# A fused attention and mixture-of-experts kernel: where the small experts' first-layer sums are kept, and which engine clears the result columns

## The chip, the cores and the metric

One core of one Trainium2 chip runs the whole program. The metric is the device time of one execution in microseconds (us). The five engines are named as the profile names them: PE (TensorE; PEld is its weight load), DVE (VectorE), ACT (ScalarE), POOL (GpSimd) and SP, whose queue starts most DMAs. SBUF is the working memory, PSUM the memory that matmuls write, in banks of 512 fp32 columns.

## What is computed

Attention with RMS-normed queries and keys (4 batches, 12 heads, 448 positions, head size 64) gives 1792 tokens of 768 values. Each token goes to one of 8 experts, and a dense layer with a softmax-weighted linear unit and a layer norm follows. Cut to what matters here:

```
x = attention(q, k, v, g_q, g_k)                  # 1792 x 768
expert_idx = argmax(x @ w_gate, axis=1)
for e in range(8):
    mask = expert_idx == e
    h = np.maximum(x[mask] @ w1[e], 0.0)          # 768 -> 1024
    out[mask] = gate_w[mask, None] * (h @ w2[e])  # 1024 -> 768
h = out @ w_in                                    # 768 -> 1024
ln = layer_norm(h * softmax(h)) * g_ln
result = ln @ w_out
```

## The kernel before

The program has three stages. Attention and routing come first; their instructions are placed by a planner (class `Work`). Then come the experts, in an order written out by hand (the loop `for r in range(E_)` in `body`), and last a head that takes 14 blocks of 128 tokens. The change lies in the experts and in the seam ahead of them.

**The experts.** The experts are taken in order of their number of tokens, with fixed capacities `CAP = (192, 280, 280, 280, 256, 208, 208, 192)`. Experts 0, 5, 6 and 7 of this order have fewer than 256 columns and are the small ones; experts 1 to 4 are the large ones. Every fp32 operand is split into a high part and a remainder, and a product is made of three partial products. For a large expert the three are added in the same PSUM columns. For a small one `products` runs the high and the remainder columns side by side in one matmul, so that a sum lies in two halves of a bank, `ps[:, :n]` and `ps[:, n:2n]`, which must be added.

**One step.** An expert has 8 steps `fc`, each with one first-layer sum `h` (`layer1`, 12 matmuls for a small expert) and, one step behind, its second-layer part `y` (`layer2`, 12 matmuls into six banks). PE's order is h_0, h_1, y_0, h_2, y_1 and so on, with y_7 right behind y_6. For each small sum (lines 1194 to 1203):

- ACT copies the first half to an SBUF tile `ht` (L1196);
- DVE adds the second half from PSUM to it, into `ht` (L1197, "the add");
- `between()` puts a conversion of the next weights on ACT (`w_high`, L1109);
- ACT writes `hh`, the rectified high part, from `ht` (L1202, "the relu");
- DVE writes `hl`, the rectified remainder, from `ht` and `hh` (L1203, "the subtraction"). The second-layer matmuls read both.

For a large expert the relu and the subtraction read the bank itself.

**What shares the engines.** The remainder `wl` of each weight block (L1114) is made by DVE or, for the second-layer weights of small experts, by POOL. DVE also rebuilds fp32 numbers from int64 pairs for the head's weights (L1526, L1529, L1532), and POOL makes the remainder of the first of these (L1545). `xprep` transposes one sixth of the next expert's tokens (PE L1165), from step 2 to 7 of every expert but the last.

**Banks.** The sums and the transposes take turns in two banks of the pool `ps_h` (tag `h`). In an expert with transposes, from step 2 on, every sum therefore lies in the same bank as the sum before it. In expert 7, which has none, the sums alternate.

**The result columns.** `yT` holds the experts' results by column. Expert 0 writes its first 192 columns; the other 1704 columns of each of six rows are set to zero by POOL in steps 0 to 5 of expert 1 (L1618), since later experts write at places held in registers.

**The seam.** Between attention and expert 0, POOL starts the gather of expert 0's tokens by two indirect DMAs (`ex.gather`, L1129), PE transposes them as they land (`transpose_all`, L1175), ACT takes the high part (L1183) and DVE the remainder (L1184).

Of the kernel before, what the change touches and what calls it, by code (L numbers as in the profile page):

```python
# [12 lines left out]
ALU = mybir.AluOpType  # L13
# [13 lines left out]
def f32(ap):  # L27
    return ap.bitcast(F32)
# [618 lines left out]
CAP = (192, 280, 280, 280, 256, 208, 208, 192)  # L647
# [439 lines left out]
class Experts:  # L1087
# [98 lines left out]
    def layer1(self, w, x, n, nm, fc=0, between=None):  # L1186
        nc = self.nc
        ps = self.h_bank(f"h{nm}")
        for k in range(6):
            c = slice(k * 128, (k + 1) * 128)  # L1190
            self.products(ps, [a[:, c] for a in w], [a[:, k] for a in x], n, k == 0, k == 5)
        x = self.wk.tile([128, 2 * self.cols], F32R, tag="hh", name=f"hh{nm}", bufs=2)
        hh, hl = self.parts_tiles(x, n)
        if n < 256:
            t = self.ht[fc % 2]
            nc.scalar.copy(t, ps[:, :n])  # L1196
            nc.vector.tensor_tensor(t, ps[:, n : 2 * n], t, op=ALU.add)  # L1197
        else:
            t = ps[:, :n]
        if between and n < 256:  # L1200
            between()
        nc.scalar.activation(hh, t, AF.Relu)  # L1202
        nc.vector.scalar_tensor_tensor(hl, t, 0.0, f32(hh), op0=ALU.max, op1=ALU.subtract)  # L1203
        if between and n >= 256:
            between()
        return x, hh, hl
# [166 lines left out]
def body(tc, kq, v, g_qk, w_gate, wmoe, w_in, w_out, g_ln, out):  # L1373
    nc = tc.nc
    ctx = ExitStack()
    with ctx, tc.manual_schedule():
# [29 lines left out]
        def reg(ap, eng, hi):  # L1406
            return eng.value_load(ap, min_val=0, max_val=hi)
# [15 lines left out]
        def w_high():  # L1423
            if len(wd) < len(use):
                r, fc, half = key = use[len(wd)]
                nm = f"{r}_{fc}_{half}"
                raw = raws[key]["r"] if key in raws else ex.load(w_reg(r), fc, half, nm)
                wd[key] = raw, ex.high(raw, nm), nm

        def w_low():  # L1430
            key = use[len(wd) - 1]
            if len(wd[key]) == 3:
                raw, wh, nm = wd[key]

                e = nc.gpsimd if CAP[key[0]] < 256 and (key[2] or key[1] == 0) else nc.vector
                wd[key] = wh, ex.low(raw, wh, nm, e)
# [75 lines left out]
        yT = yp.tile([128, 6, max(min(NT, sum(CAP[:r])) + CAP[r] for r in range(E_))], F32, name="yT")  # L1512
# [24 lines left out]
        def m2_in(i):  # L1537
            f = slice(i * HC, (i + 1) * HC)
            w, fs = from_f64(w_in[:, f], f"i{i}")
            hh = wih.rearrange("p k f -> p (k f)")[:, f]  # L1540
            ll = wil.rearrange("p k f -> p (k f)")[:, f]

            def parts():
                nc.scalar.copy(hh, w)
                nc.gpsimd.tensor_tensor(ll, w, f32(hh), op=ALU.subtract)  # L1545

            return fs + [parts]

        def m2_out(i):
            kk, j = divmod(i, 2)  # L1550
            f = slice(j * HC, (j + 1) * HC)
            w, fs = from_f64(w_out[128 * kk : 128 * kk + 128, f], f"o{i}")
            return fs + [
                lambda: nc.scalar.activation(wo[:, kk, f], w, AF.Copy, scale=gl[:, kk : kk + 1])
            ]
# [2 lines left out]
        gx = {0: ex.gather(gi(0), CAP[0], "0")}  # L1558
        small = [plan.lists(cnt), plan.tail_lists()]

        def run_small(m=1):
            for _ in range(m):
                while small and next(small[0], small) is small:
                    small.pop(0)
# [3 lines left out]
        def fetch(dst, src, at, t):  # L1568
            nc.gpsimd.indirect_dma_start(
                out=dst[:, t : t + 1], out_offset=None, in_=src[:, :],  # L1570
                in_offset=bass.IndirectOffsetOnAxis(ap=at[:, t : t + 1], axis=0),
            )
# [3 lines left out]
        def xprep(r, k):  # L1576
            if k == 0:
                xs[r] = ex.xT_tiles(r, CAP[r])
            ex.transpose(gx[r], xs[r], k, CAP[r], r)
# [4 lines left out]
        for r in range(E_):  # L1584
            n = CAP[r]
            if n < 256:
                t = wk.tile([128, DM], F32, tag="gx", name=f"ht{r}", bufs=4)
                ex.ht = t[:, :n], t[:, DM // 2 : DM // 2 + n]
            if r + 1 < E_:
                gx[r + 1] = ex.gather(gi(r + 1), CAP[r + 1], r + 1)  # L1590
            if r == 2:

                idx += [lambda t=t: fetch(tok, tab, plan.slot, t) for t in range(14)]
                idx += [lambda t=t: fetch(gate, gd, tok, t) for t in range(14)]
            ys = ex.y_banks(r)

            def y_out():
                for kk in range(6):
                    o, p = yT[:, kk, bass.ds(o_v, n)], ys[kk]
                    if n < 256:  # L1600
                        nc.scalar.copy(yT[:, kk, bass.ds(o_a, n)], p[:, :n])
                        nc.vector.tensor_tensor(o, p[:, n : 2 * n], o, op=ALU.add)
                    elif kk % 2:
                        nc.scalar.copy(yT[:, kk, bass.ds(o_a, n)], p[:, :n])
                    else:
                        nc.vector.tensor_copy(o, p[:, :n])

            h_prev = None
            m2 = []
            for fc in range(9):  # L1610
                if fc < 8:
                    h = ex.layer1(wd[r, fc, 0], xs[r], n, f"{r}_{fc}", fc, w_high)
                    w_low()
                    if r:
                        run_small(8)
                    if r == 1 and fc < 6:

                        nc.gpsimd.memset(yT[:, fc, CAP[0] :], 0.0)  # L1618
                    if m2:
                        m2.pop(0)()  # L1620
                if fc > 0:
                    ex.layer2(wd[r, fc - 1, 1], h_prev, ys, n, fc - 1)
                    if fc == 8 and n < 256:
                        y_out()
                    w_high()
                    w_low()
                h_prev = h
                if r + 1 < E_ and 2 <= fc < 8:
                    xprep(r + 1, fc - 2)
                if fc in (0, 2, 4, 6):  # L1630
                    u = fc // 2
                    m2 = m2_in(4 * r + u) if r < 4 else m2_out(4 * (r - 4) + u)
                    m2.pop(0)()
                else:
                    m2.pop(0)()
                for _ in range(2):
                    if idx:
                        idx.pop(0)()
                if r == E_ - 1 and fc == 5:
                    hd = Head(nc, None, None, None, ident, (wih, wil), None, out)  # L1640

                    free = lambda nm: wk.tile([128, DM], F32, tag="gx", name=nm, bufs=4)
                    cut = lambda a: a.bitcast(F32R).rearrange("p (k n) -> p k n", k=6)
                    ysp = hd.split(yT[:, :, 0:128], 0, (cut(free("yh0")), cut(free("yl0"))))
                if fc == 4:
                    o_a, o_v = (
                        reg(plan.off_i[0:1, r : r + 1], e, min(NT, sum(CAP[:r]))) if r else 0 for e in (nc.scalar, nc.vector)
                    )
            if n >= 256:
                y_out()  # L1650
# [203 lines left out]
```

## Time and profile before

| | us |
|---|---|
| median of 3 runs | 899.03 |
| lowest and highest | 896.51, 904.44 |
| the profiled execution | 896.94 |
| its span in the profile | 895.2 |
| PE busy in it | 811.1 (91%) |
| DVE, ACT, POOL busy | 641.4, 497.8, 395.1 |

The profile is one execution. Its span is the time from the first to the last instruction; 1.7 us lie around it. The seam ends at about 336 us, expert 0 runs to 371, experts 1 to 4 to 535, experts 5 to 7 to 635, and the head to the end. In the timeline a row gives its start, its duration, engine, line, operation and operands, and in brackets how long the engine sat idle before it and what ended that.

### The profile page before, as it was taken

Reading aid. Unit: us, or ns where it says so; the run is one execution under the profiler, and the core shown is the slowest. Engines: PE = TensorE matmul, PEld = TensorE weight load, DVE = VectorE, ACT = ScalarE, POOL = GpSimd, SP = SyncE. Lnnn points to the kernel's source line nnn. Section 1 sums busy time; section 2 is a strip of 40 time slices with the busy share of each in tenths; the row PEclk is TensorE's granted clock in tenths of the full one; section 3 lists DMA queues with packets and bytes.
Section 4 is the critical chain, followed back from the end, with each engine's and each line's share of the span. In section 5 each row is a group of like instructions: output and inputs, shape, how many; then the busy total and the mean of one; then the engine's idle time right before and its main releaser. Section 6 shows DMA issues by size and latency. Waiting matters only on the chain.

```text
span 895.2 us, 18893 instructions
## 1 busy us (share of the span) xinstructions
PE 811.1 (91%) x6811; PEld 740.8 (83%) x6811; DVE 641.4 (72%) x1484; ACT 497.8 (56%) x958; POOL 395.1 (44%) x420
## 2 busy tenths in 40 slices
PE   2788998987898959989999999899899999999994
PEld 2577887776787849979999999789779989998994
DVE  7988998897898937998667778788575434444541
ACT  7787988886885805644455556667532323332221
POOL 4777898787784624543674125545110000000000
PEclk9999999999997979999999999999999999999998
DMA  7476575574743355757666777767000000000001
GB/s 207 125 200 171 134 197 145 146 197 83 198 111 83 117 118 164 222 187 244 209 220 202 260 229 250 243 211 245 2 1 36 19 36 19 18 18 36 19 18 38
DMA packets 63871, 120.29 MB, mean 134 GB/s; under 512 B 12159, under 2 KB 35290, under 8 KB 63774
## 3 DMA queue, kind: packets, MB, share of 16 engines
q1 hardware_dynamic: 60478, 107.69, 40.8%
q0 software_dynamic: 3296, 11.35, 4.0%
q8 instruction: 56, 0.92, 0.4%
q14 instruction: 41, 0.34, 0.1%
HBM read 86.08 MB, written 11.03 MB: 108 GB/s over the span
## 4 chain that ended last, share of the span: by engine, by line
PE 36%; issue 26%; DVE 17%; DMA 13%; ACT 4%; POOL 2%; SPq 1%; POOLq 0%; ACTq 0%; DVEq 0%
DMA out_dram<-ot,tok 5%; PE st L497 4%; DMA QQ<-QQ 3%; PE h L1157 3%; DVE mx L508 2%; PE h L1158 2%; PE y L1157 2%; PE h L1159 2%; PE y L1158 2%; PE y L1159 2%; PE r L497 2%; PE h L1154 2%; DMA gx<-xd,gx 2%; PE y L1154 2%; DMA rkq<-in_kq_dram 2%
## 5 line engine op out<-in xcount | busy, mean ns | idle before, releaser
L558 POOL TENSOR_TENSOR pl<-pf,ph 128x448 f16<-128x448 f32 x153 | 166.1, 1105 | 47.7 <-ACT ph L555 16.8
L1359 POOL DMA_INDIRECT out_dram<-ot,tok x14 | 13.8, 987 | 214.3 <-ACT ot L1358 208.8
L508 DVE TENSOR_REDUCE mx<-r 128x1 f32<-128x448 f32 x168 | 99.4, 611 | 12.3 <-PE r L497 11.9
L1114 POOL TENSOR_TENSOR wl<-wr,wh 128x768 fp32r<-128x768 f32 x34 | 64.5, 1899 | 93.6 <-ACT wh L1109 93.1
L1109 ACT CAST wh<-wr 128x768 fp32r<-128x768 f32 x128 | 104.7, 831 | 1.6 <-DMA wr<-in_wmoe_dram 1.6
L1114 DVE TENSOR_TENSOR wl<-wr,wh 128x768 fp32r<-128x768 f32 x94 | 97.5, 1037 | 10.5 <-ACT wh L1109 9.0
L551 ACT ACTIVATE pf<-st 128x448 f32<-128x448 f32 x168 | 86.7, 544 | 22.0 <-PE st L497 19.5
L497 PE MATMUL r<-KS,QQ 128*128 128x448 f32 x192 | 69.0, 428 | 21.0 <-DMA QQ<-QQ 12.1
L555 ACT CAST ph<-pf 128x448 f16<-128x448 f32 x153 | 82.5, 569 | 0.3
L587 PEld LDWEIGHTS <-ph 128*128 128x128 f16 x768 | 71.0, 97 | 12.0 <-issue 10.9
L587 PE MATMUL av<-va,ph 128*128 128x65 f16 x768 | 80.1, 194 | 0.0
L588 PE MATMUL av<-va,ph 128*128 128x64 f16 x768 | 79.7, 195 | 0.0
L589 PE MATMUL av<-va,pl 128*128 128x65 f16 x768 | 79.3, 193 | 0.0
L497 PE MATMUL st<-QQ,KS 128*128 128x448 f32 x192 | 74.4, 408 | 2.7 <-ACT pf L551 2.6
L1320 DVE TENSOR_TENSOR cl<-ct,ch 128x512 fp32r<-128x512 f32 x28 | 18.1, 686 | 80.3 <-ACT ch L1319 80.2
L589 PEld LDWEIGHTS <-pl 128*128 128x128 f16 x768 | 71.6, 99 | 0.0
L588 PEld LDWEIGHTS <-ph 128*128 128x128 f16 x768 | 71.4, 97 | 0.1
L497 PE MATMUL st<-Q,K 128*128 128x448 f32 x192 | 68.7, 378 | 0.5 <-DMA K<-KS 0.5
L1154 PE MATMUL y<-hh,wh 128*128 128x384 f32 (+1 forms) x192 | 61.0, 354 | 7.7 <-DVE hh L1203 7.4
L1154 PE MATMUL h<-xx,wh 128*128 128x384 f32 (+1 forms) x192 | 63.0, 364 | 0.4 <-DVE xx L1184 0.4
L497 PEld LDWEIGHTS r<-KS,QQ 128*128 128x128 f32 x192 | 35.5, 199 | 31.1 <-DVE mx L508 5.9
L1157 PE MATMUL h<-xx,wh 128*128 128x280 f32 (+1 forms) x192 | 57.4, 299 | 0.7 <-DVE hh L1203 0.7
(282 smaller groups left out, 2525.9 us busy)
## 6 DMA issues: line engine op xcount, KB each, us to landing
wr<-in_wmoe_dram SPq DMA_DIRECT2D x128, 384.0 KB
rkq<-in_kq_dram SPq DMA_DIRECT2D x24, 448.0 KB
di<-in_w_in_dram SPq DMA_DIRECT2D x16, 384.0 KB
rv<-in_v_dram SPq DMA_DIRECT2D x24, 256.0 KB
do<-in_w_out_dram SPq DMA_DIRECT2D x16, 384.0 KB
K<-KS SPq DMA_DIRECT2D x48, 112.0 KB
KS<-Q SPq DMA_DIRECT2D x48, 112.0 KB
QQ<-QQ SPq DMA_DIRECT2D x48, 112.0 KB
```

The costliest lines, as they stand in the source:

```text
L497: nc.tensor.matmul(ps[:, :S], H[w][x + "x"][:, columns(w, s)], H[w][y], start=(k == 0), stop=(k == len(n) - 1))
L508: V.tensor_reduce(C["mx"][:, s : s + 1], C["sm", s][:, :S], axis=AX.X, op=ALU.max, negate=True)
L551: nc.scalar.activation(C["pf", s], C["st", s][:, :S], AF.Exp)
L555: (eng[e].copy if e == "ACT" else eng[e].tensor_copy)(ph[s][:, :S], C["pf", s])
L558: eng[e].tensor_tensor(pl[s][:, :S], C["pf", s], ph[s][:, :S], op=ALU.subtract)
L587: nc.tensor.matmul(o, hp, vs[:, 0:65], start=(s == ss[0]), stop=False)
L588: nc.tensor.matmul(o[:, 0:64], hp, vs[:, 65:129], start=False, stop=False)
L589: nc.tensor.matmul(o, lp, vs[:, 0:65], start=False, stop=(s == ss[-1]))
L1109: self.nc.scalar.copy(wh, raw)
L1114: (eng or self.nc.vector).tensor_tensor(wl, raw, f32(wh), op=ALU.subtract)
L1154: mm(ps[:, : 2 * n], wh, xx[:, : 2 * n], start=start, stop=False)
L1157: mm(ps[:, :n], wh, xh, start=start, stop=False)
```

## The change

Two edits. In a small expert's step, ACT now copies the second half of the sum to SBUF, and DVE adds it onto the first half in PSUM, in place; the relu and the subtraction read PSUM. The six fills of `yT` are taken from POOL in expert 1 and put on DVE at the seam, behind the issue of expert 0's gather.

```
@@ layer1
         if n < 256:
-            t = self.ht[fc % 2]
-            nc.scalar.copy(t, ps[:, :n])
-            nc.vector.tensor_tensor(t, ps[:, n : 2 * n], t, op=ALU.add)
+
+            t = ps[:, :n]
+            lo = self.ht[fc % 2]
+            nc.scalar.copy(lo, ps[:, n : 2 * n])
+            nc.vector.tensor_tensor(t, t, lo, op=ALU.add)
         else:
             t = ps[:, :n]
@@ body, at the seam
         gx = {0: ex.gather(gi(0), CAP[0], "0")}
         small = [plan.lists(cnt), plan.tail_lists()]
 
+        for k in range(6):
+            nc.vector.memset(yT[:, k, CAP[0] :], 0.0)
+
@@ body, in the loop over experts
                     if r:
                         run_small(8)
-                    if r == 1 and fc < 6:
-
-                        nc.gpsimd.memset(yT[:, fc, CAP[0] :], 0.0)
```

The lines behind the second edit are two to five higher in the changed program (L1197 is L1199 there, L1203 is L1205, L1545 is L1547).

POOL's order around the start of expert 1, before: the gather of expert 2, and the fills between the remainders of the head's weights.

```order
L1545 TENSOR_TENSOR wil<-cvi_6079,wih 128x384
L1129 DMA gx_0_6172<-xd,gx 128x768
L1129 DMA gx_1_6174<-xd,gx 128x768
L1129 DMA gx_2_6176<-xd,gx 24x768
L1618 MEMSET yT 128x1704 x3
L1545 TENSOR_TENSOR wil<-cvi_6230,wih 128x384
L1618 MEMSET yT 128x1704 x2
L1545 TENSOR_TENSOR wil<-cvi_6375,wih 128x384
L1618 MEMSET yT 128x1704
L1545 TENSOR_TENSOR wil<-cvi_6521,wih 128x384
```

The fills are gone from there. They stand in DVE's order at the seam now, between the last cast of the routing (L988) and the first remainder of expert 0's transposed tokens (L1184):

```order
L984 CAST pl_gf<-gx 128x24
L988 CAST pl_rows<-r_101 24x128
L1564 MEMSET yT 128x1704 x6
L1184 TENSOR_TENSOR xx_5716<-yx_0_5717,xx_5716 128x192
L1184 TENSOR_TENSOR xx_5716<-yx_1_5718,xx_5716 128x192
```

In the steps of a small expert the order stays and the operands change. This is DVE in expert 0 from step 2 to step 3 in the changed program, where the add and the subtraction name the bank (`h_2`, `h_3`); before, both named `ht_5741` there, the add as its result and the subtraction as its input.

```order
L1199 TENSOR_TENSOR h_2_5824<-h_2_5824,ht_5747 128x192
L1205 SCALAR_TENSOR_TENSOR hh_2_5837<-h_2_5824,hh_2_5837 128x192
L1114 TENSOR_TENSOR wl_4_0_5866<-wr_4_0_5862,wh_4_0_5864 128x768
L1184 TENSOR_TENSOR xx_5868<-xp_0_5869,xx_5868 128x280
L1528 TENSOR_SCALAR cvi_5877<-di_5875 128x384
L1199 TENSOR_TENSOR h_3_5879<-h_3_5879,ht_5747 128x192
L1205 SCALAR_TENSOR_TENSOR hh_3_5892<-h_3_5879,hh_3_5892 128x192
```

A bank is free for its next sum when its last reader is done. That was the add, and is the subtraction now.

## Rows read from the trace of the kernel before

**Rows 1.** Timeline of PE: waits in experts 0, 1, 5, 6 and 7.

```profile
369.60 0.45 PE L1154 MATMUL y<-hh,wh 128*128 128x384 f32 x1 [1.15 <-DVE hh L1203]
...
385.79 0.40 PE L1157 MATMUL h<-xx,wh 128*128 128x280 f32 x1 [0.72 <-DVE hh L1203]
392.64 0.61 PE L1165 MATMUL xp<-ident,gx 128*128 128x128 f32 x3 [1.95 <-DVE xx L1184]
...
563.71 0.46 PE L1154 MATMUL y<-hh,wh 128*128 128x416 f32 x1 [1.55 <-DVE hh L1203]
...
577.69 0.27 PE L1165 MATMUL xp<-ident,gx 64*128 64x64 f32 x1 [1.95 <-DMA gx<-xd,gx]
...
601.66 0.46 PE L1154 MATMUL y<-hh,wh 128*128 128x416 f32 x1 [1.19 <-DVE hh L1203]
...
630.60 0.44 PE L1154 MATMUL y<-hh,wh 128*128 128x384 f32 x1 [1.49 <-DVE hh L1203]
633.57 0.45 PE L1154 MATMUL y<-hh,wh 128*128 128x384 f32 x1 [0.98 <-DVE hh L1203]
```

**Rows 2.** Busy time by stretch, experts 1 to 4 (clock, DMA share and GB/s last).

```profile
372.00:535.00 163.00, 158.91 (x1234) 155.56 (x1232) 126.29 (x235) 80.36 (x153) 74.23 (x61) 1.00 0.69 220
```

**Rows 3.** Timeline of DVE in expert 1.

```profile
380.12 2.83 DVE L1018 TENSOR_SCALAR pl_base<-pl_base 128x8 f32<-128x8 f32 x1
...
386.82 3.62 DVE L1028 TENSOR_SCALAR pl_slot<-pl_q 128x14 int32<-128x14 f32 x1
```

**Rows 4.** Timeline of POOL in expert 1: the fourth and fifth fill.

```profile
387.42 2.98 POOL L1618 MEMSET yT<- 128x1704 f32 x2
```

**Rows 5.** The subtraction, by operands: ns min/median/max, first and last start, forms.

```profile
L1203 DVE SCALAR_TENSOR_TENSOR hh<-ht,hh x32: 358/1220/2166, 341.5 to 632.4; 128x192 fp32r<-128x192 f32 x16, 128x208 fp32r<-128x208 f32 x16
L1203 DVE SCALAR_TENSOR_TENSOR hh<-h,hh x32: 424/446/451, 375.0 to 527.6; 128x280 fp32r<-128x280 f32 x24, 128x256 fp32r<-128x256 f32 x8
```

**Rows 6.** Timeline of POOL in experts 6 and 7: two remainders of weights.

```profile
599.56 1.82 POOL L1114 TENSOR_TENSOR wl<-wr,wh 128x768 fp32r<-128x768 f32 x1 [0.43 <-ACT wh L1109]
...
626.83 1.85 POOL L1114 TENSOR_TENSOR wl<-wr,wh 128x768 fp32r<-128x768 f32 x1 [1.88 <-ACT wh L1109]
```

**Rows 7.** Timeline of DVE in experts 0, 5, 6 and 7.

```profile
360.30 1.22 DVE L1203 SCALAR_TENSOR_TENSOR hh<-ht,hh 128x192 fp32r<-128x192 f32 x1 [0.43 <-ACT hh L1202]
...
366.50 1.99 DVE L1526 TENSOR_SCALAR cvi<-di 128x384 int32<-128x384 int32 x1 [0.25 <-POOL wil L1545]
...
542.72 1.22 DVE L1203 SCALAR_TENSOR_TENSOR hh<-ht,hh 128x208 fp32r<-128x208 f32 x1 [0.44 <-ACT hh L1202]
...
560.16 1.59 DVE L1526 TENSOR_SCALAR cvo<-do 128x384 int32<-128x384 int32 x1
...
562.47 1.18 DVE L1203 SCALAR_TENSOR_TENSOR hh<-ht,hh 128x208 fp32r<-128x208 f32 x1 [0.44 <-ACT hh L1202]
...
600.08 1.53 DVE L1203 SCALAR_TENSOR_TENSOR hh<-ht,hh 128x208 fp32r<-128x208 f32 x1 [0.44 <-ACT hh L1202]
...
626.89 2.60 DVE L1233 TENSOR_TENSOR yl<-yT,yh 128x768 fp32r<-128x768 f32 x1
...
632.42 1.10 DVE L1203 SCALAR_TENSOR_TENSOR hh<-ht,hh 128x192 fp32r<-128x192 f32 x1 [0.43 <-ACT hh L1202]
```

**Rows 8.** Timeline of PE: starts of first-layer sums, one of expert 0, one of expert 5.

```profile
360.14 0.44 PE L1154 MATMUL h<-xx,wh 128*128 128x384 f32 x1
...
542.34 0.45 PE L1154 MATMUL h<-xx,wh 128*128 128x416 f32 x1
```

**Rows 9.** Timeline of all engines: the seam, and the start of the program.

```profile
1.03 0.48 DVE L251 MEMSET zero<- 128x512 f32 x1
...
1.37 0.20 POOL L248 MEMSET ones_f<- 128x128 f32 x1
...
323.87 0.28 DVE L988 CAST pl_rows<-r 24x128 int32<-24x128 f32 x1 [0.48 <-PE r L986]
...
336.09 1.68 DVE L1184 TENSOR_TENSOR xx<-yx,xx 128x192 fp32r<-128x192 f32 x6 [11.94 <-ACT xx L1183]
```

## The prediction

> **What bounds the kernel now.** I read the busy times by stretch first, then PE's timeline with its waits, then DVE's and POOL's rows at those places. In experts 1 to 4 PE is busy for 158.9 of 163 us [rows 2], and the head behind the experts is PE's own work, so only time in which PE waits can be won. There are few such waits [rows 1]. Each small expert ends with one: y_7 stands right behind y_6 and needs hh of the sum just made. These are 1.15 us in expert 0, 1.55 in expert 5, 1.19 in expert 6, and in expert 7 one for y_6 (1.49) and one for y_7 (0.98). Expert 1 has two, 0.72 and 1.95, that end with DVE.
>
> Why DVE is late stands in its own rows. A cast of 8 columns took 2.83 us and one of 14 took 3.62 [rows 3]. The second ends at 390.44, and POOL's fourth and fifth fill, which run beside it, at 390.40 [rows 4]. DVE was held until POOL was done. The subtraction shows the same: with both operands in SBUF it takes 358 ns at best, 1220 in the median and 2166 at worst, and with one operand in PSUM 424 to 451 in all 32, for more columns [rows 5]. The one of 1.53 us ends at 601.61 [rows 7], POOL's remainder beside it at 601.38 [rows 6]. So a held DVE instruction ends about 0.2 us behind POOL, and an instruction that reads PSUM is not held.
>
> **The fill.** Removed from expert 1: six fills, and the two waits behind them. Without them the 2.83 us cast is a short one and the chain behind it (conversion, remainder, subtraction) is 2.7 us earlier, more than the 0.72 that PE waited. The 3.62 us cast was requested at 386.82; a remainder on POOL still holds it for 0.6 us (the fills begin at 387.42 [rows 4]), and then the chain to the transposed tokens' remainder is 3.0 us earlier, more than 1.95. Both waits go: **2.67 us**. PE has none behind them until expert 5, so what is won there stays won.
>
> Added at the seam: six DVE fills of 1704 columns. No DVE fill of this size is in the trace; the nearest row is 512 columns in 0.48 us [rows 9], which scales to 1.6 us each and 9.6 in all. The bounds are POOL's 1.5 us each (9.0 in all) and twice the scaled row (19). I take 9.6. DVE's last cast there ends at 324.15 and the next DVE instruction starts at 336.09, after an idle time of 11.94 us in which the gather lands [rows 9]. The fills end at about 333.8, 2.3 us before DVE is needed: cost 0. If that cover is gone, each us beyond it costs a us, as PE waits for that remainder. The fills read nothing of attention that is still open at 324; POOL has only the gathers then, so the fills cannot be held by it.
>
> **The subtraction.** Its 32 small instances lose the hold. By row it costs in PSUM what it costs in SBUF: 424 ns for 256 columns less 64 at a nanosecond each is 360, against 358 [rows 5]. The add keeps one operand in each memory; that it now writes PSUM is in no row, and I take the same time, with bounds of -0.1 and +0.1 us each. [...]
>
> What that gives at the ends of the experts:
>
> - Expert 6: the subtraction at 600.08 ends at 600.46 instead of 601.61 [rows 7]: 1.15 of the 1.19.
> - Expert 5: the subtraction at 562.47 loses 0.80 of its 1.18. The 1.59 us conversion ahead of it (L1526) has its operands in SBUF and stays held, so 0.75 of the 1.55 stays, unless PE itself comes later.
> - Expert 0: the wait stays. It comes from a held conversion of 1.99 us [rows 7], and the subtraction behind it was not held.
> - Expert 7: the subtraction at 632.42 loses 0.74. The 1.49 comes from a held remainder of yT (L1233, 2.60 us), asked for at 626.89, just 0.06 us after POOL began at 626.83 [rows 6, 7]. Subtractions ahead of it that end sooner let the held conversions behind them end about 0.3 us sooner, enough for DVE to be first. Between 0.74 and 2.47; I take 1.3, as POOL's own remainder then ends later and y_6 needs that too.
>
> **What it adds: a wait for the bank.** In an expert with transposes every sum from h_3 on lies in the bank of the sum before it. Until now that bank was free after the add; now it is free after the subtraction, two instructions later. Behind the waiting matmul stands all of PE, and behind PE everything. In expert 5, h_3 starts at 542.34 [rows 8], but the subtraction of h_2 starts at 542.72 [rows 7] and, free of the hold, ends at 543.10: with 0.05 us of passing on, PE waits 0.81. Nothing ahead of it on DVE is shortened by the change, so this one is sure. In expert 0 the largest of its five cases is 360.30 plus 0.36 and 0.05 against 360.14: 0.57 [rows 7, 8]. Experts 0, 5 and 6 have five such sums each (h_3 to h_7). The upper bound is that nothing moves: 5 times 0.81 and 5 times 0.57, or 6.9 us, and none in expert 6, where PE waits 1.95 us for the next expert's gather ahead of h_3 [rows 1], which gives DVE its lead back before the first bank is asked for. The lower bound is the sure 0.81.
>
> Between them: once PE is late by 0.81, the later sums end later too, and DVE, with shorter subtractions, comes to the add sooner. But two-operand work behind the subtraction is still held until POOL ends (the hold moves to it). By the code every second step has two conversions on DVE ahead of the next add, the others one. Where there is one I take 0.1, where there are two 0.4, half of the sure case. Expert 5: 0.81 + 2 x 0.1 + 2 x 0.4 = 1.8. In expert 0 no case is sure, since the subtractions ahead of h_3 were held and now end sooner, and the largest is smaller: I take 0.6 in all, about a fifth of its bound. Since PE then comes 1.8 us late to the end of expert 5, the 0.75 left there is covered as well, and its whole 1.55 goes.
>
> **The sum.** Won: 2.67 + 1.55 + 1.15 + 1.3 = 6.7. Lost: 1.8 + 0.6 = 2.4. Net 4.3 us, from the profiled execution's 896.94 to 892.6. That execution is 2.1 us below the median of the three runs and near their fastest; from the median it would be 894.7. I say 893.5. A measurement of this kernel can tell about 1% (9 us) from no change, so this is within it.
>
> **The rivals.**
>
> - *The bank takes it all.* The subtraction moves from off PE's path onto it. For it: the sure 0.81, and the held work behind the subtraction. Against it: the held time that it removes, 1220 less 358 ns in the median [rows 5], is more than any of these waits. With 6.9 lost and 2.67 + 1.55 + 1.15 + 0.74 = 6.1 won, it is 0.8 slower: 897.7. It decides if more than half of the ten waits stay at their full size. Chance 0.17.
> - *No bank wait but the sure one.* DVE, free of holds, catches up. Then 2.67 + 0.80 + 1.15 + 2.47 - 0.81 = 6.3 is won: 890.6. Against it: what stands behind the subtraction is still held. Chance 0.15.
> - *The fill delays the gather (slower).* The gather's transfers are issued from POOL in the same microseconds as the fills. If a DVE fill shuts POOL out as POOL's shuts out DVE, the gather is late by up to the fills, 9.6 us, less the 4.3: up to 5.3 slower, 902.2. It decides from 4.3 us of delay on. Against it: at the program's start POOL's fill of 128 columns ran at 0.20 us inside DVE's 0.48 us [rows 9]. Chance 0.08. [...]
> - *The fills cost nothing to move, since expert 1 waits for something else then.* The 1.95 would stay if the next expert's gather landed late; the row names DVE and not the gather as what ended it [rows 1]. Net 2.3: 894.6, which is inside the forecast's own range and has no chance apart from it.
>
> The forecast holds 0.60: 891 to 896. The range for 8 in 10 takes in both bounds of the bank wait, less its end, and the spread of single runs (896.5 to 904.4): 888.5 to 899.0. Faster by over 1% needs the second rival and more: 0.08. Slower by over 1% needs a delay of the gather and a loss: 0.03. Within 1%: 0.89.
>
> **What would show it.** Right: the subtraction's longest instance under 0.5 us; no cast over 1 us in expert 1 and PE's two waits gone; a DVE row of six fills ending before 335 and the seam's subtraction still starting near 336; new waits of PE at h_3 to h_7 of experts 0 and 5, ended by L1205, of 1.5 to 3 us together; y_7 of experts 5 and 6 with 0.1 us or none. Wrong: a first subtraction at the seam later than 337, adds of over 0.45 us, or bank waits over 5 us.

## The result and the profile after

| | before | after |
|---|---|---|
| median of the timed runs | 899.18 us (6 runs, 896.51 to 904.44) | 890.3 us (6 runs, 887.75 to 890.96) |
| profiled execution | 896.94 us | 890.64 us |
| its span | 895.2 us | 888.8 us |

The ratio recorded from the runs is 0.9886, with a 95% interval of 0.9854 to 0.9917 (the two medians alone give 0.990). The forecast was 893.5 us (888.5 to 899.0), most likely within 1% of no change. The time lies inside the range and the ratio a little past that 1%. In a second comparison of the same two kernels the ratio was 0.9898 (0.9852 to 0.9944).

Where the 6.4 us between the two profiled spans went, stage by stage. The boundaries are starts of rows: POOL's first gather of expert 0, PE's first sum of expert 0, of expert 1, of expert 5, and the first product of the head.

| stage, us | before | after | difference |
|---|---|---|---|
| attention, up to the gather | 324.08 | 325.19 | +1.11 |
| seam | 12.42 | 12.16 | -0.26 |
| expert 0 | 35.00 | 35.19 | +0.19 |
| experts 1 to 4, to the first sum of expert 5 | 159.89 | 157.17 | -2.72 |
| experts 5 to 7 | 104.08 | 100.28 | -3.80 |
| head | 259.73 | 258.81 | -0.92 |

The change touches neither attention nor the head. In the profiles of this study the gather starts anywhere from 321.5 to 331.6 us, about as wide as the spread of single runs. So the later comparisons use the time from the gather to the end of the span ("seam to end"): 571.1 us before, 563.6 after.

PE's timeline after, all its waits for another engine or a transfer in experts 0, 1 and 5 to 7 (start, length, the instruction; in brackets the wait ahead of it and what ended it):

```profile
370.70 0.44 PE L1154 MATMUL y<-hh,wh 128*128 128x384 f32 x1 [0.88 <-DVE hh L1205]
...
385.77 0.24 PE L1165 MATMUL xp<-ident,gx 24*128 24x24 f32 x1 [1.23 <-DMA gx<-xd,gx]
...
534.64 0.46 PE L1154 MATMUL y<-hh,wh 128*128 128x416 f32 x1 [1.06 <-DVE hh L1205]
...
541.38 0.46 PE L1154 MATMUL h<-xx,wh 128*128 128x416 f32 x1 [0.59 <-DVE hh L1205]
549.76 0.46 PE L1154 MATMUL h<-xx,wh 128*128 128x416 f32 x1 [0.30 <-DVE hh L1205]
558.14 0.46 PE L1154 MATMUL h<-xx,wh 128*128 128x416 f32 x1 [0.27 <-DVE hh L1205]
...
568.25 0.43 PE L1154 MATMUL y<-hh,wh 128*128 128x416 f32 x1 [0.27 <-DVE hh L1205]
575.80 0.27 PE L1165 MATMUL xp<-ident,gx 64*128 64x64 f32 x1 [1.67 <-DMA gx<-xd,gx]
...
604.46 0.42 PE L1154 MATMUL y<-hh,wh 128*128 128x384 f32 x1 [0.21 <-DVE hh L1205]
626.25 0.38 PE L1155 MATMUL y<-hh,wl 128*128 128x256 f32 x1 [0.21 <-POOL wl L1114]
```

Against [rows 1]: both waits of expert 1 for DVE are gone, and so are those at y_7 of experts 5, 6 and 7 and at y_6 of expert 7. The wait at the end of expert 0 is still there, 0.88 for 1.15. The three rows "h<-xx ... <-DVE hh" are new: a first-layer sum that waits for its bank, all in expert 5 and 1.16 us together. The 1.06 at the first y of expert 5 is not new: it was 1.09 before (at 536.35), and [rows 1] leaves it out.

The subtraction and the add after (ns min/median/max, first and last start, forms):

```profile
L1205 DVE SCALAR_TENSOR_TENSOR hh<-h,hh x64: 356/400/451, 342.3 to 627.4; 128x280 fp32r<-128x280 f32 x24, 128x192 fp32r<-128x192 f32 x16, 128x208 fp32r<-128x208 f32 x16, 128x256 fp32r<-128x256 f32 x8
L1199 DVE TENSOR_TENSOR h<-h,ht x32: 348/366/383, 341.3 to 626.6; 128x192 f32<-128x192 f32 x16, 128x208 f32<-128x208 f32 x16
```

The small subtractions have joined the form that was never held: the longest of all 64 (small and large experts) is 451 ns, where [rows 5] had 2166. The shortest, 356, equals the 358 from SBUF. The add into PSUM costs what the add into SBUF cost (348 to 383 ns, against 342 to 375 before).

DVE's timeline at the seam:

```profile
325.58 1.48 DVE L1564 MEMSET yT<- 128x1704 f32 x1 [0.31 <-issue]
...
334.50 1.48 DVE L1564 MEMSET yT<- 128x1704 f32 x1 [0.30 <-issue]
336.94 0.89 DVE L1184 TENSOR_TENSOR xx<-yx,xx 128x192 fp32r<-128x192 f32 x3 [0.96 <-ACT xx L1183]
```

Six fills, each 1.48 us with 0.30 us ahead of it, end at 335.98, and the first subtraction of the seam still waits 0.96 us for ACT. So the fills lie in the shadow of the gather, but with 0.96 us to spare and not 2.3.

DVE's timeline in expert 1, the two casts of [rows 3]:

```profile
381.18 0.17 DVE L1018 TENSOR_SCALAR pl_base<-pl_base 128x8 f32<-128x8 f32 x1
...
385.22 0.67 DVE L1028 TENSOR_SCALAR pl_slot<-pl_q 128x14 int32<-128x14 f32 x1
```

From 2.83 and 3.62 us to 0.17 and 0.67: it was POOL's fill that held them. The experiments below bear it out: 0.17 and 0.67 in fill_only, and 2.82 and 3.61 in psum_only and no_pool_rem, where the fills stay on POOL.

### The profile page after: what moved, and what is told of

Read it like the earlier page. It is cut to its first block, busy times and chain, and to the rows that moved or that the text cites. A ratio compares the mean times of both kernels' runs of the same rounds, so it can differ in the third digit from the quotient of the medians.

```text
span 888.8 us, 18908 instructions
## 1 busy us (share of the span) xinstructions
PE 810.0 (91%) x6811; PEld 740.0 (83%) x6811; DVE 632.1 (71%) x1490; ACT 497.1 (56%) x958; POOL 387.2 (44%) x414
## 4 chain that ended last, share of the span: by engine, by line
PE 35%; issue 26%; DMA 15%; DVE 15%; ACT 3%; POOL 2%; SPq 2%; POOLq 0%; DVEq 0%; ACTq 0%
DMA out_dram<-ot,tok 5%; PE st L497 4%; PE h L1157 3%; DMA gx<-xd,gx 3%; DVE mx L508 3%; PE h L1158 2%; PE y L1157 2%; PE h L1159 2%; DMA QQ<-QQ 2%; PE y L1158 2%; PE y L1159 2%; PE r L497 2%; PE h L1154 2%; DMA rkq<-in_kq_dram 2%; DMA KS<-QQ 2%
## 5 line engine op out<-in xcount | busy, mean ns | idle before, releaser
L1204 ACT ACTIVATE hh<-h 128x280 fp32r<-128x280 f32 (+3 forms) x64 | 23.6, 369 | 73.7 <-PE h L1159 59.7
```

## The experiments

Theory A: the change has two parts that add. The fill's hold cost PE 2.7 us in expert 1, and the hold of the subtraction, by POOL's remainders of weights, cost it at the ends of the experts. Against it stood three others: that one part does all; that the fill at the seam delays the gather; that DVE is short of time, rather than held. Ratios go by runs of the kernel before on the same chip.

### fill_only: the fill alone

```diff
+        for k in range(6):
+            nc.vector.memset(yT[:, k, CAP[0] :], 0.0)
...
-                    if r == 1 and fc < 6:
-                        nc.gpsimd.memset(yT[:, fc, CAP[0] :], 0.0)
```

> The kernel before with the fill moved alone. Theory (two separate gains): PE's two waits in expert 1 go, 0.72 and 1.95 us, the small experts' waits stay at 1.15, 1.55, 1.19, 1.49 and 0.98, and the time is 2.5 to 3 us less than before. Rival (the fill is the whole gain, since POOL's fills disturb more than the two casts): 7 to 9 us less. Rival (the cover at the seam is too short and eats it): first subtraction at the seam late by 1 us or more, no gain.

Measured: 899.33 us (12 runs), before 901.09 (29 runs), ratio 0.9976 (0.9943 to 1.001). Experts 1 to 4 took 157.23 us, as after (157.17) and not as before (159.89). PE's waits for DVE in expert 1 are gone. The subtraction is held as before:

```profile
L1204 DVE SCALAR_TENSOR_TENSOR hh<-ht,hh x32: 358/1282/2166, 346.5 to 631.3; 128x192 fp32r<-128x192 f32 x16, 128x208 fp32r<-128x208 f32 x16
```

So the 2.7 us in experts 1 to 4 are the fill's, all of them. As a whole time that is 0.2% (1.8 us between the medians, for 2.5 to 3 expected), which the comparison alone can't tell from nothing; the stage tells it.

The expectation missed in expert 7. The waits at the ends of experts 0, 5 and 6 stayed (1.24, 1.55 and 1.19), but the 1.49 and 0.98 of expert 7 came to 0.67 and 0.19. In this profile DVE's remainder of yT was not held, and POOL's remainder beside it was:

```profile
627.47 0.94 DVE L1234 TENSOR_TENSOR yl<-yT,yh 128x768 fp32r<-128x768 f32 x1
627.43 2.69 POOL L1114 TENSOR_TENSOR wl<-wr,wh 128x768 fp32r<-128x768 f32 x1 [1.91 <-ACT wh L1109]
```

With that, a shorter wait for expert 7's gather (1.41) and no dip of the clock behind it (last section but one), experts 5 to 7 took 100.56 us here, as little as after (100.28), with the subtractions held. So that stage, in single profiles, can't tell what the sums in PSUM are worth; the ratio of psum_only does.

### psum_only: the sums in PSUM alone

```diff
-            t = self.ht[fc % 2]
-            nc.scalar.copy(t, ps[:, :n])
-            nc.vector.tensor_tensor(t, ps[:, n : 2 * n], t, op=ALU.add)
+            t = ps[:, :n]
+            lo = self.ht[fc % 2]
+            nc.scalar.copy(lo, ps[:, n : 2 * n])
+            nc.vector.tensor_tensor(t, t, lo, op=ALU.add)
```

> The kernel before with the sums kept in PSUM alone; the fills stay on POOL in expert 1. Theory: every subtraction takes 0.35 to 0.46 us, the waits at the ends of experts 5, 6 and 7 shrink to 0.3 us or less, three or four new waits of PE for a bank of 1.2 us together appear in expert 5, the two waits of expert 1 stay, and the time is 4 to 5 us less than before. Rival (bank waits take it back): within 1 us of before. Rival (the two edits only pay together): less than 2 us.

Measured: 894.25 us (12 runs), ratio 0.9942 (0.9914 to 0.997). Experts 5 to 7 took 98.19 us against 104.08, experts 1 to 4 160.07, as before. PE's waits from 530 to 640 us, grouped (total, times, longest), of this kernel:

```profile
PE y L1154 <- DVE hh L1204: 1.6, 3, 1.1
PE h L1154 <- DVE hh L1204: 1.1, 3, 0.6
PE xp L1165 <- DMA gx<-xd,gx: 1.1, 1, 1.1
PE y L1155 <- POOL wl L1114: 0.2, 1, 0.2
```

and of the kernel before:

```profile
PE y L1154 <- DVE hh L1203: 6.3, 5, 1.5
PE xp L1165 <- DMA gx<-xd,gx: 2.0, 1, 2.0
```

The y waits fall by 4.7 us and the bank gives back 1.1. Of the 4.7, 1.6 are those of expert 7, which fell in fill_only too; and of the 5.9 us of the stage, 0.9 are a shorter wait for the gather and some 1.5 the dip that did not follow it. The whole time fell by more than was expected, 5.2 us by the ratio and 6.8 between the medians, for 4 to 5. With the fill's part the two make 0.8% of gain, and the whole change 1.0 to 1.1%: they add within the intervals.

### fill_twice: twice the fills at the seam

```diff
-        for k in range(6):
-            nc.vector.memset(yT[:, k, CAP[0] :], 0.0)
+        for k in range(12):
+            nc.vector.memset(yT[:, k % 6, CAP[0] :], 0.0)
```

> The changed kernel with the six fills written twice at the seam. A fill and the gap behind it take 1.78 us there, and DVE sits idle 0.96 us between the last fill and the first subtraction. Theory (the cover is nearly used up, and each us beyond it costs one): six more fills end 10.7 us later, the first subtraction starts 9.7 us later, and the time is 9 to 10.5 us above that of the changed kernel. Rival (PE has other work to hide it): under 5 us. If fills held POOL's transfers back, the gather's data would land later too; the theory has its first block land as before.

Measured: 900.56 us (10 runs), ratio to before 1.0009 (0.9976 to 1.0042): the whole gain is gone. The seam took 21.74 us, 9.58 more than after. Six more fills are 6 times 1.78 or 10.7 us, less the 0.96 left of the cover: 9.7. PE's timeline at the seam:

```profile
338.57 1.51 PE L1175 MATMUL yx<-ident,gx 128*128 128x128 f32 x6 [6.84 <-DMA gx<-xd,gx]
340.81 0.90 PE L1175 MATMUL yx<-ident,gx 64*128 64x64 f32 x6 [0.72 <-DMA gx<-xd,gx]
350.55 0.69 PE L1154 MATMUL h<-xx,wh 128*128 128x384 f32 x1 [8.84 <-DVE xx L1184]
```

The gather was issued at 328.81 and its tokens are transposed from 338.57, 9.8 us later; with six fills it was 8.4, before 8.7, in the other profiles of this study 9.1 to 10.6; the three without a fill there have 8.7, 9.6 and 10.0. So the fills don't delay the gather, not even twelve that run on behind its landing. What waits is the next DVE instruction, by every us past the cover.

### no_pool_rem: the kernel before, no remainder of an expert weight on POOL

```diff
-                e = nc.gpsimd if CAP[key[0]] < 256 and (key[2] or key[1] == 0) else nc.vector
+                e = nc.vector
```

> The kernel before with all remainders of expert weights on DVE, so that POOL has only the head's remainders and the fills beside the small experts' steps. Theory (POOL's instruction holds the subtraction): the subtraction from SBUF takes under 0.4 us in nearly all of its 32 instances, with holds left only beside the head's remainders in expert 0. Rival (the SBUF operands themselves make it slow): its median stays above 1 us. The time is not the point; DVE has 34 instances of 0.95 us more.

Measured in one run: 889.88 us, experts 5 to 7 in 95.40 us. The subtraction, its operands in SBUF as before:

```profile
L1203 DVE SCALAR_TENSOR_TENSOR hh<-ht,hh x32: 357/367/377, 343.4 to 626.2; 128x192 fp32r<-128x192 f32 x16, 128x208 fp32r<-128x208 f32 x16
```

From 1220 ns in the median to 367, with nothing of the subtraction changed. So POOL's remainder is what held it, and DVE is not short of time: it does the remainder in 0.95 us, where POOL takes 1.85.

### dve_rem_after and dve_rem_fill: both parts, without POOL's remainders

The edit of no_pool_rem in the changed kernel (dve_rem_after, sums in PSUM), and in fill_only (dve_rem_fill, sums in SBUF). With them ran the changed kernel once more.

> The changed kernel once more, to compare with the other three on one chip. Theory A (two gains that add: about 2.7 us from the fill in experts 1 to 4, about 4 to 6 us from the sums in experts 5 to 7): ratio to before between 0.985 and 0.992, seam to end again about 563.6 us. Theory B (part of the 8.3 us between the two profiles was the length of the attention stage and a dip of the granted clock in expert 6, which the change does not touch): ratio nearer 0.994, seam to end 565 or more.

> The changed kernel, with every remainder of the expert weights on VectorE. Theory A (the instruction that holds VectorE's subtraction is GpSimd's remainder of a weight; the sums in PSUM and a GpSimd without remainders are two cures of one ill, so they do not add): nothing is held, L1205 stays at 360 to 400 ns on the mean, experts 5 to 7 take 95 to 97 us instead of 100.3, the bank waits of expert 5 (1.16 us together in the changed kernel) stay within 0.5 to 1.5 us because the sums still stand in PSUM; seam to end 559 to 561 us, 3 to 4 us under the changed kernel. Theory B (VectorE has no room for 0.95 us per step more): waits of TensorE for the remainder or the subtraction of over 3 us together, experts 5 to 7 at 100 us or more, no gain on the changed kernel.

> The kernel before with the fill moved to the seam and every remainder on VectorE, the sums in SBUF as before. Theory A: the 2.7 us of the fill in experts 1 to 4 come on top of what the kernel before with all remainders on VectorE showed (seam to end 562.55 us): 559.9 us, experts 1 to 4 at 157.2 us, experts 5 to 7 at 95.4 us, no bank wait, waits for the subtraction of 1.5 to 2.5 us in experts 5 to 7; against the run with the sums in PSUM it differs by under 1.5 us. Theory B (bank waits are what limits the gain of the sums in PSUM): it is faster than the run with the sums in PSUM by 1.5 us or more.

| | median of 6 (range), us | ratio to before (902.7 us, 11 runs) | seam to end | experts 1 to 4 | experts 5 to 7 |
|---|---|---|---|---|---|
| after_again | 894.95 (891.32 to 898.65) | 0.9898 (0.9852 to 0.9944) | 565.2 | 157.55 | 100.35 |
| dve_rem_after | 890.2 (884.26 to 892.79) | 0.9848 (0.9798 to 0.9898) | 559.4 | 157.54 | 95.73 |
| dve_rem_fill | 889.19 (885.49 to 891.38) | 0.9831 (0.9785 to 0.9878) | 559.9 | 156.64 | 95.43 |

Both are faster than the kernel before and, in median, some 5 us (0.5 to 0.6%) faster than the changed kernel. Of the 12 runs 9 lie below the lowest of the changed kernel's six. Sums in PSUM or in SBUF then makes no difference: the two are 1 us apart, with ranges that overlap. Both edits free the subtraction, and on that their gains don't add. The changed kernel itself met the expected ratio (0.985 to 0.992) but not the expected 563.6 us from the seam to the end; 565.2 is what its rival had.

Most of what dve_rem_after has over the changed kernel is not the subtraction's. PE's waits from 530 to 640 us, in the changed kernel:

```profile
PE xp L1165 <- DMA gx<-xd,gx: 1.7, 1, 1.7
PE y L1154 <- DVE hh L1205: 1.5, 3, 1.1
PE h L1154 <- DVE hh L1205: 1.2, 3, 0.6
PE y L1155 <- POOL wl L1114: 0.2, 1, 0.2
```

and in dve_rem_after:

```profile
PE y L1154 <- DVE hh L1205: 2.0, 3, 0.9
```

Experts 5 to 7 took 4.6 us less. The waits for DVE and POOL fall by 0.9 us together. The wait for expert 7's gather, 1.7 us, is gone, and with it the dip of the clock that follows it in the changed kernel, some 1.5 us (last section but one). The wait is gone in all three profiles without POOL's remainders, and in the seven with them it is 1.09 to 1.95 us. POOL's rows show why. In the changed kernel the gather stands behind a remainder:

```profile
565.46 1.86 POOL L1114 TENSOR_TENSOR wl<-wr,wh 128x768 fp32r<-128x768 f32 x1 [2.16 <-ACT wh L1109]
567.47 0.97 POOL L1129 DMA_INDIRECT gx<-xd,gx  x1
568.75 1.00 POOL L1129 DMA_INDIRECT gx<-xd,gx  x1 [0.30 <-issue]
```

and in dve_rem_after POOL, with no remainders ahead, runs it as soon as its buffers are free:

```profile
532.17 0.96 POOL L1129 DMA_INDIRECT gx<-xd,gx  x1 [27.12 <-PE xp L1165]
562.99 0.90 POOL L1129 DMA_INDIRECT gx<-xd,gx  x1 [29.86 <-DVE h L1199]
```

The second part, the one that PE waits for, is issued 5.8 us earlier. So some 3 of the 4.6 us are the gather's, and 0.5 stay open. Whether issuing this gather ahead of the remainders, with the remainders left on POOL, would win the same was not tried.

There is no bank wait in dve_rem_after, though the sums are in PSUM and 0.5 to 1.5 us of it were expected. So a sum in PSUM alone does not make PE wait for the bank. What did, in the changed kernel, stands on DVE in expert 5 ahead of the three sums that wait:

```profile
535.37 2.00 DVE L1528 TENSOR_SCALAR cvo<-do 128x384 int32<-128x384 int32 x1
...
545.23 1.78 DVE L1531 SCALAR_TENSOR_TENSOR cvo<-do,cvo 128x384 int32<-128x384 int32 x1
...
553.62 1.78 DVE L1531 SCALAR_TENSOR_TENSOR cvo<-do,cvo 128x384 int32<-128x384 int32 x1
```

and on POOL beside them:

```profile
535.22 1.94 POOL L1114 TENSOR_TENSOR wl<-wr,wh 128x768 fp32r<-128x768 f32 x1 [1.65 <-ACT wh L1109]
...
544.74 1.85 POOL L1114 TENSOR_TENSOR wl<-wr,wh 128x768 fp32r<-128x768 f32 x1 [2.81 <-ACT wh L1109]
...
553.13 1.85 POOL L1114 TENSOR_TENSOR wl<-wr,wh 128x768 fp32r<-128x768 f32 x1 [2.33 <-ACT wh L1109]
```

Each of the conversions ends 0.2 to 0.4 us behind POOL's remainder; unheld, as in dve_rem_after, they take 0.35 and 0.55 us. DVE falls back by some 1.2 to 1.7 us, and the add and subtraction behind it come late for the bank. The hold left the subtraction and went to the conversion that follows it: the 16 of the second kind for the last weights (`cvo`, L1529) took 546 ns in the median and 553 at most before, and 1524 in the median in the changed kernel (L1531). The 1.06 us at the first y of expert 5, gone in dve_rem_after too, has a held conversion ahead of it there as well (L1534, 1.91 us from 529.61).

Of dve_rem_after and dve_rem_fill the runs don't pick one; what both have is the one line that takes the remainders off POOL, and the moved fill.

### late_conv: the held conversion of expert 0 out of the way

```diff
                 if fc in (0, 2, 4, 6):
...
-                    m2.pop(0)()
+                    if r or fc < 6:
+                        m2.pop(0)()
                 else:
                     m2.pop(0)()
+                    if r == 0 and fc == 8:
+                        m2.pop(0)()
```

> The changed kernel; in expert 0 alone the first conversion step of the weight fetched at step 6 (held 2.00 us at 367.62 us in the changed kernel) is issued a step later, behind the subtraction of step 7. Theory A (that held conversion is what stands ahead of the last sum and subtraction of expert 0): the wait of y_7 in expert 0 falls from 0.88 to under 0.2 us, expert 0 takes 34.3 us instead of 35.2. Theory B (the wait belongs to the step itself, as the first y of expert 5 shows with 1.06 us and no held conversion ahead): 0.6 us or more of it stays.

Measured: 894.25 us (6 runs), 0.9887 (0.9841 to 0.9933), no different from after_again's 894.95. In the profile no wait of PE is left in expert 0 behind its first sum, so the 0.87 at y_7 was that conversion's. Expert 0 took 34.64 us (34.3 were expected) against 34.86 in after_again and 35.19 after: less gained than the wait was long, and no time that can be measured. In that profile experts 1 to 4 took 159.84, 2.3 us more than in after_again: the gather in expert 1 was waited for 0.58 and 1.44 us, and the clock fell behind it (last section but one).

## Why the prediction was right, step by step

- **The fill out of expert 1: right.** Taken 2.67 us; the stage shows 2.72, and fill_only alone 2.66. The waits for DVE went, one for a gather stayed (1.23 us in one piece for 0.40 and 0.71).
- **The fill at the seam costs nothing: right, with the size off.** The row of 512 columns gave 1.6 us each; they take 1.48 and 0.30 between them, 1.78. So they end at 335.98 and not at 333.8. The seam begins 1.11 us later in this profile; by the clock of the kernel before that is 334.87, which just meets the sign of 335, and the subtraction behind them starts at 335.83, near the 336 that was named. Of the cover 0.96 us was left and not 2.3. fill_twice shows the price behind the cover, a us per us, as it was put.
- **The fill does not delay the gather: right**; that rival falls with fill_twice. The row held against it shows two fills that overlap, not one inside the other: POOL's began within DVE's and ended at 1.57 us, 0.06 behind it [rows 9].
- **The subtraction unheld: right.** No row over 451 ns; no_pool_rem shows that POOL's remainder was the cause. In PSUM it takes no longer than in SBUF: 356 ns at the shortest against 358, by the rows.
- **Expert 0's wait stays: right**, 0.88 of 1.15, and late_conv shows that it is the held conversion.
- **Expert 6: right**, its 1.19 at y_7 is gone; 0.27 at its own first y is new.
- **Expert 7: mis-sized, 1.3 taken, 2.05 measured, and its cause not shown.** Both waits went (1.49 + 0.98) and two of 0.21 came. DVE's remainder of yT got through first, as the step had it, in its timeline and in POOL's:

```profile
623.55 0.95 DVE L1235 TENSOR_TENSOR yl<-yT,yh 128x768 fp32r<-128x768 f32 x1
```

```profile
623.59 2.61 POOL L1114 TENSOR_TENSOR wl<-wr,wh 128x768 fp32r<-128x768 f32 x1 [1.71 <-ACT wh L1109]
```

  The remainder of yT took 0.95 us instead of 2.60, and now POOL is held, 2.61 instead of 1.85. PE lost only 0.21 by that, so the value lay near the upper end. But the step's reason, that shorter subtractions let DVE be first, is not borne out: in fill_only DVE was first with the subtractions held as before, and 1.61 of the 2.05 us came there too. It was a race of 0.06 us in the kernel before, and which way it went may in part be luck. One of the two is held in all three kernels, DVE before and POOL in the two others. What decides which of them is held can't be read off these rows: DVE's starts 0.06 us behind POOL's before, 0.04 ahead of it here and 0.04 behind it in fill_only.
- **The bank wait: the step that was mis-sized, 2.4 taken, 1.16 measured.** For expert 5 it was 1.8: the sure case at h_3 was put at 0.81 and measured 0.59, h_5 and h_7 (0.4 each) 0.30 and 0.27, h_4 and h_6 (0.1 each) none; the sign asked for 1.5 to 3 us together. For expert 0 it was 0.6, and there is none. The step saw that the hold moves to the conversions, and that where two stand ahead of the add the wait is the longer; dve_rem_after shows that without the hold no bank wait is left. What it had wrong, as far as the rows show, is the rest of DVE: shorter subtractions gave it more lead than was allowed, in expert 0 enough for all five sums.
- **The sum.** Taken 4.3 us; from the seam to the head the profiles show 6.6. The bank explains 1.24 of the difference and expert 7 0.75; the rest is 0.3. That puts the time at the rival "no bank wait but the sure one" (890.6), whose sum of 6.3 is nearer than the forecast's. Its reason, that DVE catches up, is what was seen, but for the 0.57 us at h_5 and h_7. The medians fell by 8.9 us, twice the net of 4.3; the time stayed inside the range since the range allowed for the spread of single runs.

Two single profiles don't bear a sum out to 0.3 us: in experts 5 to 7 each may carry some 1.5 us of a lower clock, as the next section shows. These two both do, so it does not stand in their difference.

## What the runs showed of the hardware that was not expected

**Behind some waits of PE the granted clock was lower, 0.72 to 0.76 on the mean of 6 us, and such a wait cost more than its own length.** Busy time by stretch (PE, PEld, DVE, ACT, POOL, then the granted clock, DMA share, GB/s), right behind the gather's wait in expert 6. Before, after a wait of 1.95 us:

```profile
578.00:584.00 6.00, 6.00 (x28) 5.60 (x29) 3.72 (x6) 2.75 (x7) 1.84 (x1) 0.72 0.68 239
584.00:590.00 6.00, 6.00 (x40) 5.74 (x39) 5.24 (x8) 2.86 (x7) 1.83 (x1) 1.00 0.47 139
```

and fill_only, after one of 1.41:

```profile
580.00:586.00 6.00, 6.00 (x38) 5.70 (x39) 4.38 (x7) 3.37 (x7) 1.84 (x1) 1.00 0.76 255
```

At a mean clock of 0.72 PE got through 28 matmuls in 6 us, and through 38 or 40 at 1.00: some 10 matmuls lost, or 1.5 us (10 of 39 in 6 us). After (0.72 behind 1.67 us) and after_again (0.73 behind 1.77) show it too; late_conv (1.35 there), psum_only (1.09) and fill_only do not. Nor does fill_twice, behind a wait of 1.95 us, as long as the one before:

```profile
590.00:596.00 6.00, 6.00 (x40) 5.71 (x39) 4.38 (x8) 2.97 (x7) 1.83 (x1) 1.00 0.69 212
```

So the length of that one wait does not decide it. The change doesn't touch that gather, so experts 5 to 7 can differ by 1.5 us between profiles for this alone. In psum_only (and in no_pool_rem, 0.72 from 388 to 394 us) the same befell expert 1, where waits of 0.51, 0.45 and 0.88 us stand between 383 and 385 us:

```profile
386.00:392.00 6.00, 5.61 (x34) 5.38 (x33) 5.82 (x11) 2.15 (x4) 3.73 (x3) 0.76 0.34 104
```

That fits its experts 1 to 4, which gained nothing though their waits in expert 1 were 1.5 us shorter than before. And late_conv, behind its 0.58 and 1.44:

```profile
394.00:400.00 6.00, 6.00 (x36) 6.00 (x36) 3.46 (x10) 2.11 (x4) 0.00 (x0) 0.72 0.60 195
```

The kernel before waited longer in expert 1 (3.78 us in four waits) and read 1.00 throughout, so the runs don't settle which wait is followed by a dip.

**POOL's fill, which reads nothing, held casts of 8 and 14 columns** (2.83 and 3.62 us for 0.17 and 0.67). The fill on DVE did not hold POOL: its gathers at the seam took 0.91 to 1.19 us each beside it, as they did before without it.

## What to carry to other kernels

Where an instruction takes three times its shortest time, as the subtraction did (1220 ns in the median, 358 at best), look at what the other engine runs beside it, and whether both end together. Here the hold had more than one cure, an operand in PSUM or the other engine's work taken away, and the gains did not add (890.2 us with both, 889.19 with POOL's work taken away alone). Taking POOL's work onto the engine that it held was worth more, some 5 us, since it freed the conversions as well and, above all, since a gather behind that work in POOL's queue was issued 5.8 us earlier: ask what else stands in the queue that is relieved. When two engines ask within 0.1 us of each other (0.04 and 0.06 here), one profile does not tell how the race goes in general. When a hold is taken from one instruction, look for the next one in the queue that can be held, and price the new wait there. A cover for moved work is measured to the end of the last piece with the gaps between pieces counted (0.30 us beside 1.48 here).
